# The last two pairs of output blocks move from GpSimd's queue to SP's, as fp32, behind the buffers of earlier transfers

## Chip, cores, metric

One core of one Trainium2 chip. The metric is the device time of one execution in microseconds (us), the median of several runs; lower is better. Every ratio below is the mean time of one kernel's fast runs over that of the other's fast runs of the same rounds, so it is not quite the ratio of the medians that stand beside it.

Three words are used throughout. To *evacuate* a block is to copy a matmul's result out of PSUM, where matmuls leave it, into a buffer in SBUF, from which a transfer can take it. A *closing DRAIN* is an instruction that stands behind an engine's last work in the program; the profile doesn't count it as busy. The *barrier* is the last exchange of semaphores between the engines, which ends only when the last engine has come to it.

## The reference

Attention with a window (plain for four heads, dilated for four) for 8 x 8 x 576 x 64, followed by a soft mixture of experts with 32 slots. Only its last line matters here:

```python
logits = x @ phi                       # x: 4608 x 512, the attention's output
...                                    # slot_out: 32 x 512, from the experts' weights
c = logits - logits.max(1, keepdims=True)
c = np.exp(c)
c /= c.sum(1, keepdims=True) + 1e-09
return (c @ slot_out).astype(np.float32)     # 4608 x 512 fp32, 9.44 MB
```

## The kernel before

All but the end of the kernel is the same before and after. The end multiplies the exponentials `ET` (fp16, 32 slots by 4608 rows) by `so_sb` (the slots' outputs), scales each row by `rrow`, and writes. The 36 blocks of 128 rows go in pairs. Pairs 0 to 7 are written in two halves of 256 columns, because the left half of `so_sb` is ready earlier; pairs 8 to 17 are written whole. Everything is fp16 in SBUF, and GpSimd's transfers cast it to the fp32 of the output.

```python
def combine_full(pair):
    r0 = 256 * pair
    ot = out_pool.tile([128, 2, DMODEL], FP16, name=f"of_{pair}", tag="of", bufs=8)
    for k in range(2):
        blk = 2 * pair + k
        fp = psum_f.tile([128, DMODEL], FP32, name=f"f_{blk}", tag="f")
        nc.tensor.matmul(fp, ET[:, 128 * blk : 128 * blk + 128], so_sb, start=True, stop=True)
        if k == 0:
            nc.scalar.activation(out=ot[:, k, :], in_=fp, func=AF.Copy, scale=rrow[:, blk : blk + 1])
        else:
            nc.vector.tensor_scalar(out=ot[:, k, :], in0=fp, scalar1=rrow[:, blk : blk + 1],
                                    scalar2=None, op0=ALU.mult)
    nc.gpsimd.dma_start(out=out[r0 : r0 + 256, :].rearrange("(k p) n -> p k n", k=2), in_=ot)
...
    # half pairs of the left half, combine(0, pair), stand here (cut)
    for pair in range(NSPLIT // 2, NFIN // 2):            # 8 .. 17
        combine_full(pair)
        if pair >= NFIN // 2 - NSPLIT // 2:               # from 10 on: half pairs 0 .. 7, right half
            combine(1, pair - (NFIN // 2 - NSPLIT // 2))
```

The softmax here doesn't subtract the row's maximum and nothing guards it: scores larger than these inputs give would overflow.

## Time and profile before

| | before |
|---|---|
| time, median of 4 runs | 184.27 us (183.78 to 184.45) |
| span of the profiled execution | 182.06 us |
| output transfers issued by GpSimd (POOL) | 27 |
| last weights used, second copy to `so_sb` | 156.15 us |
| landing of the last output transfer | 178.99 us |
| end of POOL's long closing drain | 181.33 us |

The lines that carry the reading stand in the prediction. Three more fix the two ends of the output stage: the second copy to `so_sb`, after which no input is awaited, and POOL's last two issues. They are from the view of instructions in order of time (start, duration, engine, line, operation, what waited):

```profile
156.15 0.37 ACT L730 CAST so_sb<-so 128x256 f16<-128x256 f32 x1 [0.48 <-PE so L722]
...
171.32 0.72 POOL L802 DMA_DIRECT2D out_dram<-of  x1 [0.62 <-DMA out_dram<-of]
172.03 0.72 POOL L778 DMA_DIRECT2D out_dram<-ot  x1
```

POOL has issued all at 172.75; from there on only transfers run. I use the moment 156.15 as the origin of the end: how early it comes differs from execution to execution, and differences at the end are only comparable when counted from it. Landings are the times at which a transfer's semaphore got its last increment in the trace.

### The profile page before, as it was taken

The numbers are of one execution on the slowest core, as the hardware profiler recorded it, in microseconds if no ns is written. First come the engines' busy times: TensorE is split into PE (matmuls) and PEld (weight loads), VectorE is DVE, ScalarE is ACT, GpSimd is POOL, SyncE is SP. The second block draws the span as 40 slices with busy tenths as digits, with TensorE's granted clock in tenths as the row PEclk, the third lists the DMA queues.
The fourth block names the chain that finished last, engine by engine and source line by source line (L and its number), as shares of the span: only waits on it lengthen the run. The fifth ranks groups of instructions, "written<-read, shape, count | busy, mean of one in ns | idle before, by whom it ended". The sixth has DMA issues, their size and how long they took to land.

```text
span 182.1 us, 5580 instructions
## 1 busy us (share of the span) xinstructions
PE 143.7 (79%) x2464; PEld 85.7 (47%) x2464; DVE 107.5 (59%) x232; ACT 90.4 (50%) x162; POOL 85.2 (47%) x126
## 2 busy tenths in 40 slices
PE   0467977999999999999999999999869848784000
PEld 0234544646646756756756755746353424231000
DVE  4689776675984785885886886526050205697000
ACT  2044354657667566776776776673400205795000
POOL 7954654624534444263351345614412425999700
PEclk9999995699999699999999999999555996999555
DMA  4999999999999999999999999999999999999991
GB/s 61 197 193 208 208 210 213 203 211 217 198 211 216 201 213 217 199 212 214 202 211 214 202 217 213 216 210 214 214 214 213 195 196 183 377 403 409 410 407 32
DMA packets 29527, 40.75 MB, mean 224 GB/s; under 512 B 1856, under 2 KB 19264, under 8 KB 29504
## 3 DMA queue, kind: packets, MB, share of 16 engines
q0 software_dynamic: 29504, 40.41, 117.7%
q8 instruction: 19, 0.31, 0.6%
q14 instruction: 4, 0.03, 0.0%
HBM read 61.93 MB, written 9.44 MB: 392 GB/s over the span
## 4 chain that ended last, share of the span: by engine, by line
DMA 42%; PE 32%; ACT 7%; DVE 6%; POOL 4%; issue 4%; POOLq 1%
DMA w<-in_moe_w_dram 28%; DMA raw<-in_k_dram 10%; ACT p L293 5%; PE lg L408 5%; PE o_p L339 4%; PE sa L282 4%; DMA out_dram<-of 4%; PE sb L271 3%; PE sa L271 3%; DVE qk L245 2%; PE vb L163 2%; PE va L163 2%; PE rd L389 2%; PE u L452 2%; POOL raw L138 1%
## 5 line engine op out<-in xcount | busy, mean ns | idle before, releaser
L293 ACT ACTIVATE p<-sa 128x960 f16<-128x960 f32 (+2 forms) x24 | 21.4, 890 | 31.6 <-PE sb L282 31.1
L339 PEld LDWEIGHTS <-p 128*128 128x128 f16 (+2 forms) x544 | 19.6, 99 | 13.4 <-issue 9.4
L245 DVE STREAM_TRANSPOSE qk<-raw 128x320 uint32<-128x320 uint32 (+1 forms) x32 | 21.5, 677 | 0.3
L293 ACT ACTIVATE p<-sb 128x960 f16<-128x960 f32 (+2 forms) x24 | 21.2, 885 | 0.0
L271 PE MATMUL sa<-masks,ident 128*128 128x480 f16 (+2 forms) x48 | 14.8, 396 | 7.3 <-POOL masks L489 6.2
L236 DVE STREAM_TRANSPOSE qk<-raw 128x576 uint32<-128x576 uint32 x16 | 19.8, 1248 | 0.1
L212 POOL DMA_DIRECT2D w<-in_moe_w_dram x16 | 8.8, 554 | 21.4 <-DMA vs<-in_v_dram 9.9
L408 PE MATMUL lg<-xTd,phi 128*128 128x288 f16 x32 | 18.3, 659 | 0.0
L271 PEld LDWEIGHTS <-ident 128*128 128x128 f16 x96 | 9.3, 108 | 18.3 <-issue 7.2
L282 PEld LDWEIGHTS <-qk 32*128 32x128 f16 x832 | 12.3, 98 | 11.3 <-issue 9.1
L339 PE MATMUL o_p<-v,p 128*128 128x65 f16 (+1 forms) x288 | 16.6, 201 | 1.2 <-ACT v L172 0.7
L282 PE MATMUL sa<-qk 32*128 32x160 f16 (+4 forms) x416 | 16.2, 215 | 0.8 <-DVE qk L236 0.7
L282 PE MATMUL sb<-qk 32*128 32x160 f16 (+4 forms) x416 | 16.3, 215 | 0.0
L361 DVE TENSOR_TENSOR xd<-o_d,rc_d 128x448 f16<-128x448 f32 (+1 forms) x24 | 14.5, 602 | 0.8
L361 DVE TENSOR_TENSOR xp<-o_p,rc_p 128x448 f16<-128x448 f32 (+1 forms) x24 | 14.5, 602 | 0.8
L271 PE MATMUL sb<-masks,ident 128*128 128x480 f16 (+2 forms) x48 | 14.6, 390 | 0.3 <-ACT p L293 0.2
L219 POOL DMA_DIRECT2D w<-in_moe_w_dram x10 | 6.7, 671 | 16.2 <-DMA w<-in_moe_w_dram 9.8
L209 POOL COPY v<-v 32x1024 f16<-32x1024 f16 x8 | 8.3, 1033 | 11.7 <-DVE v L202 9.0
L163 PE MATMUL va<-vs,orders 32*128 32x256 f16 (+1 forms) x96 | 12.1, 289 | 1.0 <-ACT p L293 1.0
L412 ACT ACTIVATE ET<-lg 128x288 f16<-128x288 f32 x16 | 6.6, 410 | 12.5 <-PE lg L408 12.3
L382 ACT COPY xTp<-rp 128x576 f16<-128x576 f16 x16 | 10.4, 650 | 2.2 <-PE rp L377 2.2
L360 DVE RECIPROCAL rc_p<-o_p 128x7 f32<-128x7 f32 (+1 forms) x24 | 4.8, 198 | 10.7 <-PE o_p L339 10.0
(103 smaller groups left out, 277.2 us busy)
## 6 DMA issues: line engine op xcount, KB each, us to landing
w<-in_moe_w_dram POOLq DMA_DIRECT2D x16, 512.0 KB, 16.8
w<-in_moe_w_dram POOLq DMA_DIRECT2D x5, 1024.0 KB, 19.5
out_dram<-of POOLq DMA_DIRECT2D x10, 512.0 KB, 6.2
vs<-in_v_dram POOLq DMA_DIRECT2D x8, 512.0 KB, 16.1
raw<-in_q_dram POOLq DMA_DIRECT2D x7, 576.0 KB, 18.0
raw<-in_k_dram POOLq DMA_DIRECT2D x7, 576.0 KB, 18.5
out_dram<-ot POOLq DMA_DIRECT2D x15, 256.0 KB, 4.9
w<-in_moe_w_dram POOLq DMA_DIRECT2D x8, 256.0 KB, 9.7
```

Source lines behind the costliest of these rows:

```text
L163: nc.tensor.matmul(o.rearrange("p (h d) -> p h d", h=4), l, st[:, 0:4, D * r : D * r + D], start=(r == 0), stop=(r == DIL - 1), skip_group ...
L209: nc.gpsimd.tensor_copy(out=vL[b % NV][0:32, :, :, 0:D], in_=vD[b % NV][96:128, :, :, 0:D])
L212: nc.gpsimd.dma_start(out=w1t[e][:, 2 * i : 2 * i + 2, :].rearrange("p l f -> p (l f)"), in_=moe_w1[e, 256 * i : 256 * i + 256].rearrange( ...
L236: nc.vector.transpose(out=dst, in_=src)
L245: nc.vector.transpose(out=o, in_=i)
L271: nc.tensor.matmul(sps[h // 2][:, h % 2, 0:n], ident, bias[g], start=True, stop=False, skip_group_check=True,)
L282: nc.tensor.matmul(sps[h // 2][:, h % 2, c0 : c0 + w], kt_[32 * h : 32 * h + 32, k0 : k0 + 128, tt], qt_[32 * h : 32 * h + 32, q0 : q0 + w ...
L293: nc.scalar.activation(out=pt, in_=sps[ab][:, :, 0:n], func=AF.Exp, scale=SCALE)
L339: nc.tensor.matmul(o[p0 : p0 + np_, n, :], l, rr, start=(k == 0), stop=(k == len(jobs) - 1), skip_group_check=True,)
L361: nc.vector.tensor_tensor(out=x.rearrange("p t (h d) -> p (t h) d", h=4)[0:nq, u0:u1, :], in0=o[0:nq, 0:n, 0:D], in1=rc[0:nq, 0:n, None].b ...
L382: nc.scalar.copy(out=xTp_t[b][:, c, :], in_=rg)
L408: nc.tensor.matmul(lp, phi4[:, kc].rearrange("p c s -> p (c s)"), rhs, start=(kc == 0), stop=(kc == 3))
```

## The change

The intent: two pairs less for GpSimd's queue, without a cast, and so late that they run behind all of GpSimd's transfers. For that the two last full pairs (16 and 17) share their fp32 buffers with an earlier transfer (pair 15, half pair 5): they can only be evacuated from PSUM when that one has landed. The two last half pairs are moved ahead of them. Fewer buffers for the other tiles make room.

```diff
--- before.py
+++ after.py
@@ -761,7 +761,13 @@
                 stop=True,
                 skip_group_check=True,
             )
-        ot = out_pool.tile([128, 2, NH], FP16, name=f"ot{half}_{pair}", tag=f"ot{half}", bufs=NSPLIT // 2)
+        if (half, pair) == (1, 5):
+            ot = out_pool.tile([128, 2, DMODEL], FP32, name="last1_a", tag="last1")
+            ot = ot[:, 0, 0:NH].bitcast(FP16).rearrange("p (k n) -> p k n", k=2)
+        else:
+            ot = out_pool.tile(
+                [128, 2, NH], FP16, name=f"ot{half}_{pair}", tag=f"ot{half}", bufs=NSPLIT // 2 - half
+            )
         if pair % 2 == 0:
             for k in range(2):
                 blk = 2 * pair + k
@@ -782,7 +788,13 @@
 
     def combine_full(pair):
         r0 = 256 * pair
-        ot = out_pool.tile([128, 2, DMODEL], FP16, name=f"of_{pair}", tag="of", bufs=8)
+        if pair < NFIN // 2 - 3:
+            ot = out_pool.tile([128, 2, DMODEL], FP16, name=f"of_{pair}", tag="of", bufs=6)
+        else:
+            tag = "last1" if pair == NFIN // 2 - 1 else "last0"
+            ot = out_pool.tile([128, 2, DMODEL], FP32, name=f"ol_{pair}", tag=tag)
+            if pair == NFIN // 2 - 3:
+                ot = ot[:, 0, :].bitcast(FP16).rearrange("p (k n) -> p k n", k=2)
         for k in range(2):
             blk = 2 * pair + k
             fp = psum_f.tile([128, DMODEL], FP32, name=f"f_{blk}", tag="f")
@@ -799,7 +811,7 @@
                     scalar2=None,
                     op0=ALU.mult,
                 )
-        nc.gpsimd.dma_start(
+        (nc.gpsimd if pair < NFIN // 2 - 2 else nc.sync).dma_start(
             out=out[r0 : r0 + 256, :].rearrange("(k p) n -> p k n", k=2), in_=ot
         )
 
@@ -813,10 +825,14 @@
             if pair in at:
                 slot_out(1, (HALVED[at[pair]],))
         slot_out(1, HALVED[1:])
-        for pair in range(NSPLIT // 2, NFIN // 2):
+        for pair in range(NSPLIT // 2, NFIN // 2 - 2):
             combine_full(pair)
             if pair >= NFIN // 2 - NSPLIT // 2:
                 combine(1, pair - (NFIN // 2 - NSPLIT // 2))
+        for pair in range(2):
+            combine(1, NSPLIT // 2 - 2 + pair)
+        for pair in range(2):
+            combine_full(NFIN // 2 - 2 + pair)
     psum_f.release()
     psum_so.release()
     out_pool.release()
```

## The prediction

> **What bounds the kernel now.** I read the page first: which engine is full at the end, and what the transfers do there.
>
> ```profile
> POOL 7954654624534444263351345614412425999700
> DMA  4999999999999999999999999999999999999991
> GB/s 61 197 193 208 208 210 213 203 211 217 198 211 216 201 213 217 199 212 214 202 211 214 202 217 213 216 210 214 214 214 213 195 196 183 377 403 409 410 407 32
> ```
>
> A slice is 4.55 us. From slice 35 on the output is written at about 410 GB/s and the transfer engines are full up to slice 39; compute ends before that. Only the end can change: the change touches nothing before the output stage. Next, the end cut into stretches (columns: stretch, its length, busy time of PE, PE loads, DVE, ACT, POOL, clock, DMA share, GB/s):
>
> ```profile
> 172.00:174.00 2.00, 0.00 (x0) 0.00 (x0) 0.00 (x0) 0.00 (x0) 0.75 (x2) 0.50 1.64 407
> 174.00:176.00 2.00, 0.00 (x0) 0.00 (x0) 0.00 (x0) 0.00 (x0) 0.00 (x0) 0.50 1.64 411
> 176.00:178.00 2.00, 0.00 (x0) 0.00 (x0) 0.00 (x0) 0.00 (x0) 0.00 (x0) 0.50 1.48 361
> 178.00:179.00 1.00, 0.00 (x0) 0.00 (x0) 0.00 (x0) 0.00 (x0) 0.00 (x0) 0.50 0.19 38
> 179.00:181.40 2.40, 0.00 (x0) 0.00 (x0) 0.00 (x0) 0.00 (x0) 0.00 (x0) 0.50 0.00 0
> ```
>
> The transfers keep their pace until 177.5 and are over by 179.0, yet the span is 182.1. So some 3 us at the end belong to no transfer and no busy engine. What fills them is in two other views: SP's own waits, and the instructions of the last line of the program (the closing drains and barrier).
>
> ```profile
> SPq L851 <- DMA out_dram<-ot: 178.2, 1, 178.2
> SPq L851 <- PEq L851: 2.6, 2, 2.1
> ...
> L851 POOLq EVENT_SEMAPHORE  x4: 17/17/17, 181.4 to 182.0; - x4
> L851 POOLq DRAIN  x3: 51/86/9513, 171.8 to 181.8; - x3
> ```
>
> SP waits for the last output transfer (the trace's semaphore records put its landing at 178.99), then once more, 2.1 us, in the barrier. The view blames PE, but PE stopped at 166. The engine that comes late to the barrier is POOL: its first closing DRAIN starts at 171.81 and takes 9.513 us, so it ends at 181.33. That is 2.34 us after the last landing. SP was through its own closing waits at 179.38; the barrier then takes 0.73 us (181.33 to 182.06). The tail of 3.07 us after the last landing is therefore 0.39 (SP) + 1.95 (POOL's drain alone) + 0.73 (barrier). This, and not the 410 GB/s, is what the change can shorten.
>
> **What the Trainium skill says.** "DMA: Bandwidth & Descriptors", section "SWDGE vs HWDGE vs iDMA": a DMA that casts must be issued by GpSimd, whose software writes descriptors; DMAs from SP have theirs made by hardware. This agrees with the kernel: all output is fp16 cast to fp32 on POOL, and only fp32 buffers let SP write. Section "Issuing engines are not separate DMA queues": a second issuing engine adds no bandwidth. The trace has one queue alone, so no run yet shows it; I assume it. Section "Latency and other measured facts": first byte after about 0.6 us from SP, 1 us from GpSimd; the trace before has no transfer from SP. "VectorE: DVE Perf Modes", section "The DRAIN you can't avoid", calls the closing drains constant at about 12 ns on all engines. For SP (7 ns) that agrees, for POOL it doesn't: 9513 ns.
>
> **The change part by part.**
>
> *Bytes.* The output in HBM is fp32 both ways; two pairs are 2 x 524,288 B = 1.05 MB, at 409 GB/s 2.56 us. Reading fp32 instead of fp16 from SBUF doubles the read side only. The loads of this kernel, which read fp32 and write fp16, move 214 GB/s written, so 428 GB/s read; the read side has no lower limit than what is needed. I count no gain or loss.
>
> *POOL.* POOL issues 27 output transfers before (2, 15 and 10), 25 after. Each costs it 0.717 us, but its last issue ends at 172.75, six us before its data have landed, so that saving is hidden. What counts is that its last transfer, now the half pair 7, has 1.05 MB less in front of it: it lands at 178.99 - 2.56 = 176.4. If the drain ends 2.34 us after POOL's last landing, it ends at 178.8 instead of 181.33. The drain then lies beside SP's transfers.
>
> *The new wait.* The buffer of pair 16 is that of pair 15, the buffer of pair 17 is that of half pair 5. The trace has pair 15 landing at 174.49 and half pair 5 at 175.18; nothing ahead of them moves (the order of instructions of the changed program has the same sequence on POOL up to there). Evacuations cost as before, from the rows of that tile:
>
> ```profile
> L791 ACT ACTIVATE of<-f,rrow x10: 681/687/695, 157.0 to 165.8; 128x512 f16<-128x512 f32 x10
> L795 DVE TENSOR_SCALAR of<-f,rrow x10: 741/751/751, 157.2 to 165.9; 128x512 f16<-128x512 f32 x10
> ```
>
> Wait 0.04, then ACT 0.69 beside DVE 0.75, then 0.05 to SP: pair 16 is issued at 174.49 + 0.84 = 175.33. The second pair follows: DVE 175.28 to 176.03, issued at about 176.1, while pair 16 is still moving. From issue to first byte I take 0.6 (the skill) to 1.3 us (my doubt): 175.9 to 176.6.
>
> *The hole.* Behind pair 15 POOL's queue still holds three half pairs, 786 KB, 1.92 us. The sixteen transfer engines do not finish together: the increments of one transfer arrive over 0.9 us (175.51 to 176.41 for pair 16 before). The last data packet ends 0.4 us before its landing. So the fast engines run dry at about 175.1, the slowest at 176.0. Against a first byte at 175.9 to 176.6 the slowest engine, which sets the end, loses 0 to 0.6 us; part of the 1.92 us covers the 0.84 of evacuation and the issue.
>
> *The end.* From 176.0 to 176.6, plus 2.56 of data, plus 0.4 receipt: the last landing comes at 179.0 to 179.6, say 179.35; before 178.99. Then SP's closing waits, one more than before, 0.45; then the barrier, 0.73: 180.5. Sum against 182.06: +0.36 for the hole, +0.06 for SP's wait, -1.95 for the drain, so -1.5 us. The executions took 184.23 where the span was 182.1; carried over, 182.7. I add 0.1 for a slower start on SP and say 182.8, which is 0.8% less.
>
> *Smaller parts.* Six buffers instead of eight for full pairs: pair 14 reuses that of pair 8, which lands at 162.3, about when pair 14 is evacuated (162.2); its transfer is issued only at 165.6, so a wait of some tenths is hidden. The SP queue waits, before its first transfer, for all eight semaphores of POOL's transfers; the built program shows counts of 64 to 96 there, where the last outputs bring them to 192 or more, so these are old loads, long landed.
>
> **The rivals.** (1) *The drain doesn't shorten.* It could hold until every transfer of the core has ended, SP's too. Then the end is 179.35 + 2.34 + 0.73 = 182.4, and the time 184.6. For it: only one drain is in the trace, so I can't tell what it waits for. Against: POOL has no part in SP's descriptors. A variant, in which the drain ends a fixed 8.58 us after POOL's last issue, gives 170.7 + 8.6 = 179.3, for POOL's last issue moves forward to about 170.0 (it waits for a transfer that landed at 169.35). SP would still come later; no difference. (2) *A larger hole.* If a transfer from SP takes 2 us from issue to its first byte, the landing comes at 175.33 + 2.0 + 2.56 + 0.4 = 180.3, the end at 181.5 and the time at 183.6. For: the wait, the evacuation and the issue now stand in series where POOL had a backlog. (3) *No hole and better pace.* Transfers without a cast and without software descriptors might run at 428 instead of 409 GB/s, 0.11 us less, and hardware descriptors might level the engines' 0.9 us spread; then the landing is at 178.5 and the time at 182.0. (4) *The output stage is bandwidth bound, so nothing moves.* The page says so at first sight; against it stands the 3 us behind the last byte.
>
> **Range and chances.** Weights: main account about 0.6 (182.2 to 183.3), larger hole 0.2 (183.3 to 184.0), no drain gain 0.12 (184.2 to 184.9), better pace 0.08 (181.7 to 182.2). That gives 182.8 with 182.0 to 184.1. Faster by over 2% means under 180.6: even with the drain wholly hidden and no hole the bound is about 182, so 0.02. Slower by over 2% is over 187.9: 0.01. Within 2%: 0.97.
>
> **What the profile of the changed kernel would show.** Right: POOL's long DRAIN ends near 178.8, before SP is through its waits; ACT and DVE wait for a DMA before each of their last two evacuations; GB/s dips near 175.5 to 176.5; the last landing at 179.0 to 179.6 is of a transfer from SP; the span is near 180.5, with some 1.2 us behind the last landing. Wrong: a DRAIN that ends 2.3 us after SP's landing (rival 1), or a dip of over 1 us in the transfers (rival 2). The whole account fails if the drain's length has to do with neither the landing nor the issue of POOL's last transfer.

## The result

| | before | changed |
|---|---|---|
| median of 4 runs each | 184.27 us | 183.05 us (182.48 to 183.20) |
| ratio, 95% interval | | 0.9932 (0.9904 to 0.9961) |
| span of the profiled execution | 182.06 | 181.38 |
| `so_sb` complete | 156.15 | 156.71 |
| POOL's last landing | 178.99 | 177.11 |
| end of POOL's drain | 181.33 | 179.37 |
| SP's last landing | none | 180.35 |
| `so_sb` to last landing | 22.84 | 23.64 |
| last landing to end | 3.07 | 1.02 |

The changed kernel is 0.7% faster, about 1.25 us (0.0068 of 184.3). Within a margin of 2% that is "the same", but the interval excludes 1. Two further samples on other occasions, in the experiments, gave 0.9896 and 0.9931. The two last rows of the table account for it: +0.80 and -2.05, together -1.25 us.

The page of the changed kernel, the lines that answer to the first ones of the prediction:

```profile
POOL 7954473633633265163371337434401443999600
DMA  4999999999999999999999999999999999999996
GB/s 60 196 196 207 205 212 212 203 211 215 200 213 215 201 212 213 203 212 213 203 211 216 201 215 215 212 212 213 215 213 215 196 196 171 329 386 410 407 319 231
...
q1 hardware_dynamic: 544, 1.05, 1.6%
```

The slices are 4.53 us now. The last slice, nearly empty before (32 GB/s), carries 231 GB/s: the transfers reach closer to the end of the span. The slice ahead of it has fallen from 407 to 319: there is a hole. A second queue has appeared with the 1.05 MB of the two pairs. The hole, cut finer (same columns as in the prediction; the DMA share adds up the packets' times, so it is over 1 where the packets of one transfer engine overlap):

```profile
174.00:175.50 1.50, 0.00 (x0) 0.00 (x0) 0.24 (x1) 0.26 (x1) 0.00 (x0) 0.50 1.93 397
175.50:176.50 1.00, 0.00 (x0) 0.00 (x0) 1.00 (x2) 1.00 (x2) 0.00 (x0) 0.50 0.79 155
176.50:177.00 0.50, 0.00 (x0) 0.00 (x0) 0.17 (x1) 0.08 (x1) 0.00 (x0) 0.50 0.05 8
177.00:178.00 1.00, 0.00 (x0) 0.00 (x0) 0.00 (x0) 0.00 (x0) 0.00 (x0) 0.50 1.00 365
178.00:179.50 1.50, 0.00 (x0) 0.00 (x0) 0.00 (x0) 0.00 (x0) 0.00 (x0) 0.50 1.02 382
```

While ACT and DVE evacuate (175.5 to 176.5, both 1.00 us busy), most transfer engines have run dry, and when SP's transfers come they move 365 to 382 GB/s, not 409. The order of events at the end, from the view in order of time:

```profile
167.98 0.72 POOL L814 DMA_DIRECT2D out_dram<-ol  x1 [0.35 <-issue]
168.69 0.72 POOL L784 DMA_DIRECT2D out_dram<-last_a  x1
169.88 1.43 POOL L784 DMA_DIRECT2D out_dram<-ot  x2 [0.47 <-issue]
175.24 1.34 ACT L803 ACTIVATE ol<-f,rrow 128x512 f32<-128x512 f32 x2 [9.46 <-DMA out_dram<-ol]
175.26 1.41 DVE L807 TENSOR_SCALAR ol<-f,rrow 128x512 f32<-128x512 f32 x2 [9.10 <-DMA out_dram<-ol]
176.09 1.04 SPq L814 DMA_DIRECT2D out_dram<-ol  x2
```

The first line is pair 15, whose landing (175.13) lets ACT and DVE go on after 9.46 and 9.10 us of waiting. SP's two issues follow at 176.09 and 176.75; the first packet starts at 177.01. The closing instructions (count, shortest/median/longest in ns, first and last start):

```profile
L867 SPq EVENT_SEMAPHORE  x8: 17/28/28, 177.2 to 181.3; - x8
...
L867 POOLq DRAIN  x3: 51/91/8817, 170.5 to 181.0; - x3
L867 SPq DRAIN  x3: 7/7/7, 180.4 to 180.7; - x3
```

POOL's long drain starts at 170.55, takes 8.817 us and is over at 179.37, one microsecond before SP's last landing. SP goes through its own closing waits by 180.49 and the barrier follows at once. Before, SP stood 2.1 us in that barrier.

### The profile page after: what moved, and what is told of

It is laid out like the page before. It is cut to its first block, busy times and chain, and to the rows that moved or that the text cites. A ratio compares the mean times of both kernels' runs of the same rounds, so it can differ in the third digit from the quotient of the medians.

```text
span 181.4 us, 5591 instructions
## 1 busy us (share of the span) xinstructions
PE 145.3 (80%) x2464; PEld 86.9 (48%) x2464; DVE 107.3 (59%) x232; ACT 90.6 (50%) x162; POOL 83.7 (46%) x124
## 2 busy tenths in 40 slices
DMA packets 29527, 40.75 MB, mean 225 GB/s; under 512 B 1856, under 2 KB 19264, under 8 KB 29504
## 3 DMA queue, kind: packets, MB, share of 16 engines
q1 hardware_dynamic: 544, 1.05, 1.6%
## 4 chain that ended last, share of the span: by engine, by line
DMA 44%; PE 33%; DVE 6%; ACT 5%; POOL 5%; issue 3%; DVEq 0%; POOLq 0%
DMA w<-in_moe_w_dram 28%; DMA raw<-in_k_dram 10%; PE o_p L339 5%; PE lg L408 5%; PE sa L282 4%; ACT p L293 4%; DMA out_dram<-ol 4%; PE sa L271 4%; PE sb L271 4%; DMA out_dram<-ot 3%; DVE qk L245 2%; PE rd L389 2%; PE vb L163 2%; PE va L163 2%; PE u L452 2%
## 5 line engine op out<-in xcount | busy, mean ns | idle before, releaser
L212 POOL DMA_DIRECT2D w<-in_moe_w_dram x16 | 8.8, 552 | 18.5 <-DMA vs<-in_v_dram 7.4
L271 PE MATMUL sb<-masks,ident 128*128 128x480 f16 (+2 forms) x48 | 15.1, 403 | 0.2 <-ACT p L293 0.2
L219 POOL DMA_DIRECT2D w<-in_moe_w_dram x10 | 6.7, 670 | 15.8 <-DMA w<-in_moe_w_dram 11.3
L227 POOL DMA_DIRECT2D w<-in_moe_w_dram x8 | 6.0, 748 | 11.5 <-DMA w<-in_moe_w_dram 11.5
```

What stands on the lines that cost most here:

```text
L212: nc.gpsimd.dma_start(out=w1t[e][:, 2 * i : 2 * i + 2, :].rearrange("p l f -> p (l f)"), in_=moe_w1[e, 256 * i : 256 * i + 256].rearrange( ...
L271: nc.tensor.matmul(sps[h // 2][:, h % 2, 0:n], ident, bias[g], start=True, stop=False, skip_group_check=True,)
```

## The experiments

The theory: *the gain is POOL's closing drain, which ends some 2.3 us after the landing of POOL's last transfer; the change puts that time beside SP's transfers. The new wait costs, through the hole.* The rivals: the gain comes from SP's queue or the missing cast itself; or from the order of writing; or the drain's length is fixed by POOL's last issue and not by a landing; or the drain waits for all transfers. All outputs were correct. Twelve runs; each ratio is to the kernel before on the same chip. The table at the end of this section gathers them.

### Own buffers: the deferral undone

Against the changed kernel (`w1t` holds weights that are no longer needed):

```diff
-            ot = out_pool.tile([128, 2, DMODEL], FP32, name=f"ol_{pair}", tag=tag)
+            if pair > NFIN // 2 - 3:
+                ot = w1t[pair - (NFIN // 2 - 2)][:, 0:2, :].bitcast(FP32)
+            else:
+                ot = out_pool.tile([128, 2, DMODEL], FP32, name=f"ol_{pair}", tag=tag)
```

> Only the deferral is undone: pairs 16 and 17 get fp32 buffers of their own (in memory of dead weights), so SP can issue them at about 167 instead of 176. Theory (the gain is POOL's closing drain, which ends 2.3 us after POOL's last landing, moved beside SP's transfers): SP's 1.05 MB now travel early, among POOL's, and POOL's last landing moves back to the end of all transfers, about 179.0 to 179.6; the drain ends at about 181.6, the span at 182.0 to 182.6, the time is 184.0 to 184.5, ratio to before 1.00: the gain is lost although the hole of 1.2 us in the transfers is gone. Rival (the gain comes from the hardware queue or the missing cast, the wait only costs): the hole is gone, time about 182, ratio 0.988.

Measured: 184.78 us, ratio 1.0016 (0.9995 to 1.0037). The gain is lost, as the theory said. SP issues at 167.91 and its last transfer lands at 178.33; POOL's last one lands at 180.19. The closing instructions of this run:

```profile
L870 POOLq DRAIN  x3: 51/91/11709, 170.7 to 182.9; - x3
L870 SPq DRAIN  x3: 7/7/7, 180.4 to 182.7; - x3
```

170.74 + 11.71 = 182.45, which is 2.25 us (before rounding) after POOL's last landing, and 10.9 us after its last issue ended (171.60). SP was done at 180.5 and stood in the barrier. So fp32, SP's queue and two POOL issues fewer gain nothing by themselves. What the deferral buys is that POOL is finished first.

### POOL issues the deferred pairs: the queue undone

```diff
-        (nc.gpsimd if pair < NFIN // 2 - 2 else nc.sync).dma_start(
+        nc.gpsimd.dma_start(
```

> Only the queue is undone: the last two pairs stay fp32 and deferred, but POOL issues them. Theory: POOL's last landing is now the last of all, about 180.3; the drain ends 2.3 us later, about 182.6, the span at 183.3, the time about 185.0, ratio 1.004: slower than before by the hole. Variant (the drain ends a fixed 8 us after POOL's last issue, which is at about 177.5 here): drain to 185.6, time about 188. Rival (SP's queue has no part in the gain, the order of writing has): time about 183.1.

Measured: 186.22 us, ratio 1.0100 (1.0071 to 1.0129), slower than expected by 1.2 us. The drain behaves as the theory has it:

```profile
L867 POOLq DRAIN  x3: 51/86/6432, 177.2 to 184.1; - x3
L867 SPq DRAIN  x3: 7/7/7, 181.6 to 183.9; - x3
```

177.18 + 6.43 = 183.61, 2.34 us after the landing at 181.27. POOL's last issue ended at 178.01, 5.6 us before, against 8.6 in the kernel before: a drain fixed by the issue is out. What I had mis-sized is the hole: POOL takes up the issue only at 176.55 (SP at 176.09), its first packet comes 1.30 us after that (SP's 0.92), and between its two landings lie 1.49 us for 512 KB, where a full queue needs 1.28.

### All full pairs by SP

```diff
-        ot = out_pool.tile([128, 2, DMODEL], FP16, name=f"of_{pair}", tag="of", bufs=8)
+        i = pair - NSPLIT // 2
+        ot = w1t[i // 2][:, 2 * (i % 2) : 2 * (i % 2) + 2, :].bitcast(FP32)
...
-        nc.gpsimd.dma_start(
+        nc.sync.dma_start(
```

(against the kernel before)

> All ten full pairs are fp32 in buffers of their own and issued by SP as soon as they are evacuated, without any deferral; the half pairs stay with POOL. Theory: POOL's share ends well before SP's, so its drain is over by the time SP's last transfer lands, and there is no hole: last landing at 179.0 to 179.6, then 0.15 and the barrier 0.85, span 180.0 to 180.6, time 181.7 to 182.3, ratio 0.988. If SP's transfers run at 384 GB/s, as its two did in the changed kernel, against 409 of POOL's, 5.2 MB of them cost up to 0.9 us more: 182.6. Rival (deferral is needed for the gain): 184 or more.

Measured: 185.09 us, ratio 1.0036 (1.0010 to 1.0061). This expectation failed. I had thought that POOL, with the smaller share, would be done well ahead of SP; the trace has POOL's last landing at 180.58 and SP's at 180.45. The two queues ran side by side to the very end, so POOL's drain (end at 182.51) was exposed. Also the pace fell: 390, 387, 375 and 373 GB/s in four slices of the output, against 403 to 410 before. It is the deferral, or whatever else makes POOL finish first, that matters, not how few bytes POOL has.

### The whole output by SP

As above, with the half pairs in fp32 and by SP too (the same edit for the two single blocks of pair 0):

```diff
-        ot = out_pool.tile([128, 2, NH], FP16, name=f"ot{half}_{pair}", ...
+        ot = out_pool.tile([128, 2, NH], FP32, name=f"ot{half}_{pair}", ...
...
-        nc.gpsimd.dma_start(
+        nc.sync.dma_start(
```

> The whole output is fp32 and issued by SP, in the order of the kernel before, without deferral; POOL issues no output at all. Theory: POOL's last landing is then a load, at about 156, its drain is long over, and the end is SP's last landing plus about 1.0 us. If transfers from fp32 by SP keep the 414 GB/s that they showed in the run with earlier buffers (1.05 MB in 2.53 us), the last landing is at about 179.0 to 179.9, the time 182.2, ratio 0.988. If they run at the 383 GB/s of the changed kernel (1.37 us for 512 KB), 9.4 MB take 1.5 us more and the time is 183.7. If the two mixed queues alone made the run with all full pairs on SP slow (373 to 390 GB/s), the first number holds.

Measured: 184.14 us, ratio 0.997 (0.9938 to 1.0002). POOL's last landing is a load at 156.72, and the end comes 1.22 us after SP's last landing at 181.47: no drain in the tail. But that landing comes 24.25 us after `so_sb`, 1.4 us later than in the kernel before, and takes most of the gain back. The second of the three expectations comes nearest (the slow pace, even slower than I took it), and as there is one queue alone, it is not the mixing of two that makes it. The pace in this run, over stretches of 5 us:

```profile
165.00:170.00 5.00, 2.64 (x12) 0.96 (x11) 3.66 (x6) 3.16 (x7) 0.00 (x0) 1.00 1.03 363
170.00:175.00 5.00, 0.00 (x0) 0.00 (x0) 0.00 (x0) 0.00 (x0) 0.00 (x0) 0.53 1.04 370
```

### Earlier buffers

Pair 16 takes the buffer of pair 14, pair 17 that of pair 15; half pair 5 gets an ordinary buffer back.

```diff
-        if (half, pair) == (1, 5):
+        if False:
...
-        if pair < NFIN // 2 - 3:
+        if pair < NFIN // 2 - 4:
             ot = out_pool.tile([128, 2, DMODEL], FP16, name=f"of_{pair}", tag="of", bufs=6)
...
-            tag = "last1" if pair == NFIN // 2 - 1 else "last0"
+            tag = f"last{pair % 2}"
...
-            if pair == NFIN // 2 - 3:
+            if pair < NFIN // 2 - 2:
```

(and `bufs=NSPLIT // 2` for the half pairs)

> Deferral stays, but the buffers come free earlier: pair 16 takes the buffer of pair 14 and pair 17 that of pair 15 (landings at 173.3 and 175.1 instead of 175.1 and 175.8). Theory: the hole closes, SP's last landing comes about 0.9 us earlier, at 179.4; but SP's pair 16 now shares the engines with POOL's last half pairs, whose last landing moves from 177.1 to about 178.0, and its drain ends at about 180.3: span 181.1, time 182.8; so most of the closed hole is given back to the drain. If the drain had no part in it the time would be 182.1.

Measured: 182.18 us, ratio 0.9875 (0.9851 to 0.9898). The hole is closed, and nothing is given back. The stretches that answer to those of the changed kernel:

```profile
175.50:176.50 1.00, 0.00 (x0) 0.00 (x0) 0.72 (x1) 0.64 (x1) 0.00 (x0) 0.50 1.64 404
176.50:177.00 0.50, 0.00 (x0) 0.00 (x0) 0.00 (x0) 0.00 (x0) 0.00 (x0) 0.50 1.08 399
177.00:178.00 1.00, 0.00 (x0) 0.00 (x0) 0.00 (x0) 0.00 (x0) 0.00 (x0) 0.50 1.06 410
...
L867 POOLq DRAIN  x3: 51/91/8864, 170.7 to 180.4; - x3
```

My account of POOL's last landing was wrong: I expected SP's pair 16 to delay it by 0.9 us, to 178.0; it landed at 177.31, 20.35 us after `so_sb`, against 20.40 in the changed kernel. SP issued at 174.48, yet its first packet started at 175.95: it stood behind most of what POOL had already queued, and shared with the rest only up to POOL's last packet at 176.91. So POOL's drain ended at 179.57, still ahead of SP's last landing at 179.84. (In the run with own buffers the same shows more strongly: issued at 167.91, first packet at 171.57.) SP's last landing comes 22.88 us after `so_sb`; before it was 22.84. All of the 3.07 us behind the last landing but 0.88 is gone, and no byte comes later.

### The order alone

The two last half pairs ahead of the two last full pairs, all else as before:

```diff
-        for pair in range(NSPLIT // 2, NFIN // 2):
+        for pair in range(NSPLIT // 2, NFIN // 2 - 2):
             combine_full(pair)
             if pair >= NFIN // 2 - NSPLIT // 2:
                 combine(1, pair - (NFIN // 2 - NSPLIT // 2))
+        for pair in range(2):
+            combine(1, NSPLIT // 2 - 2 + pair)
+        for pair in range(2):
+            combine_full(NFIN // 2 - 2 + pair)
```

> One part of the change alone: the two last half pairs go ahead of the two last full pairs; all stay fp16, issued by POOL, no shared buffers. Every theory in which SP's queue or the drain makes the gain expects the time of before, ratio 1.00 within 0.003; if the order made the gain, 0.993.

Measured: 184.23 us, ratio 0.998 (0.9950 to 1.0009). The interval holds 1 and excludes the 0.993 of the rival. The trace agrees: 22.80 us from `so_sb` to the last landing and 3.07 to the end, as before.

### The changed kernel again

No edit.

> The changed kernel once more, to stand beside the others on the same chip: ratio 0.993.

Measured: 182.84 us, ratio 0.9896 (0.9869 to 0.9923), a little lower than the first 0.9932; the intervals overlap. Its trace repeats the first (23.62 and 1.02 us).

### Three pairs by SP

Pairs 15, 16 and 17 by SP, in buffers of pairs 12, 13 and 14; the half pairs 5, 6 and 7 ahead of them. The core of the edit, against the changed kernel:

```diff
-        if pair < NFIN // 2 - 3:
-            ot = out_pool.tile([128, 2, DMODEL], FP16, name=f"of_{pair}", tag="of", bufs=6)
+        if pair < NFIN // 2 - 6:
+            ot = out_pool.tile([128, 2, DMODEL], FP16, name=f"of_{pair}", tag="of", bufs=4)
...
-            tag = "last1" if pair == NFIN // 2 - 1 else "last0"
+            tag = f"last{pair % 3}"
...
-        (nc.gpsimd if pair < NFIN // 2 - 2 else nc.sync).dma_start(
+        (nc.gpsimd if pair < NFIN // 2 - 3 else nc.sync).dma_start(
```

> Three full pairs go by SP, deferred to the buffers of pairs 12, 13 and 14. Theory: in the run with earlier buffers the drain (end at 179.6) was already hidden behind SP's last landing (179.8), so hiding it deeper gains nothing: the end is set by the bytes of all transfers plus 1.0 us, time 182.2, ratio 0.987 to 0.989, with the drain ending near 178.5. If the drain still cost something there, 181.8 or less.

Measured: 182.86 us, ratio 0.9899 (0.9861 to 0.9936). No better than two pairs with earlier buffers, as the theory has it (the median is 0.6 us above what I wrote, the interval holds my range). One detail was off: the drain ended at 179.53, not near 178.5. SP's first transfer did hold up POOL's last one here: it landed 20.25 us after `so_sb`, hardly sooner than the 20.35 with two pairs on SP, although a whole pair, 1.28 us of data, had left POOL's queue.

### POOL with uncast fp32, and POOL with deferred casts

Two runs to learn whether the slow pace is SP's queue, the missing cast, or the start from idle engines. The first is the run "the whole output by SP" with POOL as the issuer of all output transfers:

```diff
-        nc.sync.dma_start(
+        nc.gpsimd.dma_start(
```

The second is the run "POOL issues the deferred pairs" with those pairs in fp16:

```diff
-            if pair == NFIN // 2 - 3:
-                ot = ot[:, 0, :].bitcast(FP16).rearrange("p (k n) -> p k n", k=2)
+            ot = ot[:, 0, :].bitcast(FP16).rearrange("p (k n) -> p k n", k=2)
```

> The whole output is fp32 in SBUF as in the run with all output on SP, but POOL issues it. It measures the pace of uncast transfers by themselves: 407 to 411 GB/s in the middle of the output if the cast makes no difference and SP's queue was the slow part (367 there); about 367 if reading fp32 from SBUF is the slow part. The drain is exposed as before: time about 184.6 at the first pace (ratio 1.00), about 187 at the second (2.4 us more for 9.4 MB).

Measured: 188.50 us, ratio 1.0217 (1.0191 to 1.0244). Pace:

```profile
165.00:170.00 5.00, 0.99 (x5) 0.29 (x3) 2.10 (x4) 1.47 (x4) 2.82 (x5) 0.86 1.01 338
170.00:175.00 5.00, 0.00 (x0) 0.00 (x0) 0.00 (x0) 0.00 (x0) 3.12 (x6) 0.50 1.01 351
```

Without the cast the transfers are slower, on POOL's queue (338 to 351 GB/s) still more than on SP's (363 to 370). It is the slowest run; whether by over 2% is unclear, as its interval holds 1.02. The cast is not all that differs: without it POOL's queue moved the same bytes in fewer, larger packets. From the pages of the kernel before and of this run (packets, MB, share):

```profile
q0 software_dynamic: 29504, 40.41, 117.7%
q0 software_dynamic: 25152, 40.41, 108.5%
```

And a transfer engine has one packet under way on the mean (DMA share 1.01 here, 1.03 and 1.04 by SP), where with the cast it has 1.64 (the stretches in the prediction). By SP the packets stayed as they were with the cast (29528 in all, 29527 before), so their size is no part of what makes SP slower. On POOL's queue no run separates it from the cast.

> As the run in which POOL issues the two deferred pairs, but these are fp16 and cast, as all others. It separates the two causes of the slow pace after the hole (1.37 us for 512 KB with SP, 1.49 with POOL, against 1.28 in a full queue): 1.28 between the last two landings if the missing cast is slow, 1.4 or more if starting from idle engines is. The time: 0.1 to 0.3 us below that of the fp32 variant (186.2), so about 186.0, ratio 1.009, as the drain is exposed and the hole is there. If the fp32 transfers themselves made the loss of that run, about 184.5.

Measured: 185.94 us, ratio 1.0084 (1.0056 to 1.0111). Between the last two landings, after the hole, lie 1.22 us, where the fp32 variant had 1.49. So on POOL's queue the start from idle engines costs no pace; the missing cast, with the packets that go with it, does. The time is 0.28 us below that of the fp32 variant, as expected, but the two ran on different occasions and their intervals overlap, so this rests on the traces; the rest of the loss is the hole and the exposed drain (2.34 us after the last landing again).

### Earlier buffers against the changed kernel, side by side

No new edit.

> The variant with earlier buffers once more, on one chip with the changed kernel, to settle whether it is the faster of the two. From the traces (last arrival of weights to the end: 23.8 us there, 24.7 us in the changed kernel) it should be 0.9 us faster than the changed kernel: ratio to before about 0.987.

> The changed kernel beside it: ratio to before 0.990 to 0.993, some 0.9 us slower than the variant with earlier buffers.

Measured, on one chip: 182.21 us, ratio 0.9873 (0.9852 to 0.9893) with earlier buffers; 183.14 us, ratio 0.9931 (0.9883 to 0.9980) for the changed kernel. The two intervals touch, but every execution of the first (181.86 to 182.40) is below every one of the second (182.47 to 184.77). The medians differ by 0.93 us, as the traces said. The version with earlier buffers is the fastest.

### All runs, counted from `so_sb`

For one profiled execution of each kernel (the three repeats, left out, agree with these in A + B within 0.14 us): A, from the start of the second copy to `so_sb` to the last landing; B, from there to the end; the difference of A + B to the kernel before (25.91); and the timed difference, ratio minus 1 times 184.6 us. Last column: end of POOL's long drain minus POOL's last landing.

| run | A | B | A+B against before | timed | drain after landing |
|---|---|---|---|---|---|
| before | 22.84 | 3.07 | | | 2.34 |
| changed | 23.64 | 1.02 | -1.25 | -1.26 | 2.26 |
| own buffers | 23.12 | 3.01 | +0.22 | +0.30 | 2.25 |
| POOL issues the deferred, fp32 | 24.56 | 3.23 | +1.88 | +1.85 | 2.34 |
| POOL issues the deferred, cast | 24.30 | 3.23 | +1.62 | +1.55 | 2.34 |
| all full pairs by SP | 24.05 | 2.72 | +0.86 | +0.66 | 1.93 |
| whole output by SP | 24.25 | 1.22 | -0.44 | -0.55 | (1.24, a load) |
| earlier buffers | 22.88 | 0.88 | -2.15 | -2.31 | 2.26 |
| order alone | 22.80 | 3.07 | -0.04 | -0.37 | 2.34 |
| three pairs by SP | 22.97 | 1.02 | -1.92 | -1.86 | 2.22 |
| whole output fp32 by POOL | 27.01 | 3.07 | +4.17 | +4.01 | 2.34 |

Read column B first: it is about 1 us where SP lands last and POOL's drain is hidden, and 2.7 to 3.2 us in every other run. Column A then tells what was paid for it. The two together give the timed difference within 0.35 us in each row.

## Why the prediction was right

The prediction said 182.8 us (range 182.0 to 184.1), 0.8% less; measured were 183.05 us, 0.7% less. The mechanism is the one that it named; the size of the hole is not, and that the number came so near is in part luck, as the sum below shows. Its steps:

- **The tail, not the bandwidth, is what the change can shorten: shown.** The 3.07 us behind the last landing became 1.02. In the run with own buffers, with the same bytes on the same queues, they came back as 3.01.
- **The drain ends 2.34 us after POOL's last landing: shown,** with 1.93 to 2.34 in ten kernels whose POOL transfers land between 177.1 and 183.2. The rival that it depends on the issue falls with the run in which POOL issued last at 178.01 and drained 5.6 us later, and with own buffers, 10.9 us later. The rival that it waits for all transfers falls with the changed kernel itself: the drain ended at 179.37 while SP's landing came at 180.35.
- **POOL's last landing moves forward by 2.56 us: right,** 20.40 us after `so_sb` instead of 22.84, so 2.44.
- **The hole: right in kind, too small in size.** The term was +0.36; A rose by 0.80. Its parts: counted from `so_sb`, SP issues 0.2 us later than I worked out. The first packet started 0.92 us after the issue, in the middle of the 0.6 to 1.3 I allowed. From the first packet to the last landing it took 3.34 us where I had put 2.96 (2.56 of data and 0.4 of receipt). The prediction had 23.20 us from `so_sb` to the last landing (179.35 less 156.15) and its rival 2, the larger hole, 24.15; measured were 23.64, about midway. One of its signs of rival 2, a dip of over 1 us in the transfers, is there too: 155 GB/s from 175.5 to 176.5 and 8 to 177.0. But rival 2's reason, 2 us from SP's issue to its first packet, is not: that was 0.92.
- **"I count no gain or loss" for fp32 against fp16: wrong, and part of the 0.38 us just named.** I argued from the loads, which read fp32 from HBM and not from SBUF, that reading fp32 cannot be the limit. After the same hole, with POOL as issuer, two cast pairs took 3.11 us from the first packet to the last landing (177.61 to 180.72), two fp32 pairs 3.42 (177.85 to 181.27). So a start after the hole takes some 0.15 more than 2.96 even with the cast, and about 0.2 of the 0.38 goes with fp32; this is an estimate, as no run has SP move cast data. The run of the whole output in fp32 moves 363 to 370 GB/s by SP and 338 to 351 by POOL, where cast transfers move 407 to 411 (the stretches of the kernel before in the prediction). Rival 3 of the prediction, a better pace without the cast, has its sign reversed in these runs.
- **The end after the last landing: 1.18 predicted** (0.45 for SP's closing waits, 0.73 for the barrier), **1.02 measured.** Most of SP's closing waits were over before its last landing came: 0.15 us remained, and the barrier took 0.88.
- **The smaller parts: right.** Pair 14's evacuation waited 0.26 us for its buffer, at 163, and its transfer was issued at 166.19 behind POOL's other issues. SP's wait for eight semaphores was long met.

The sum: -1.5 + 0.1 was predicted, -2.05 + 0.80 = -1.25 measured. The hole was 0.44 us larger and the tail shrank 0.16 us more than I had it; these two misses, and the 0.1 put on for SP, partly cancel.

Two things stay open. Why POOL's drain needs about 2.3 us after the landing, no run tells. And uncast transfers are slow in a steady stream, but SP's two fp32 pairs in the run with earlier buffers are not: 1.29 and 1.24 us per 512 KB from landing to landing, and the repeated run had 1.25 between its two. In the changed kernel the same two transfers need 1.35 to 1.37. The runs differ in how far apart the sixteen engines are when the transfers begin (increments of one transfer spread over 0.94 us there, 0.23 here; 0.44 with three pairs, at 1.25 to 1.28 us). The trace of the whole output by SP goes the same way: pairs 8 and 9 land 1.28 us after the transfer ahead of them, with spreads of 0.80 and 0.71, pairs 15, 16 and 17 need 1.40 to 1.44 with 0.33 to 0.44; pair 12, 1.76 with 0.76, falls out of the row. The cast pairs after the hole need only 1.22 at a spread of 0.19, and fp32 by POOL is slow at spreads of 1.1 to 2.3 us too, so the spread alone is not it. Whether it is the cause for SP I did not test.

## What to carry to other kernels

Look at what lies behind the last landing before working on the transfers: here 3 us of a 182 us span, of which 2 were one engine's closing drain and invisible in every busy time. When the last transfer of a kernel is on GpSimd's queue, try to let another queue carry the last stretch of data (two pairs, 2.56 us, did here against a drain that ends 2.3 us after GpSimd's landing), and see that GpSimd's own transfers land first. A transfer that is held back so that it comes last should be released while the other queue still has more than its evacuation and start-up ahead of it (here about 1.9 us, from the landing that releases it to its first packet); otherwise part of the gain goes into a hole.

## What the Trainium skill lacked or had wrong

- "VectorE: DVE Perf Modes", section "The DRAIN you can't avoid", calls the closing drains constant at about 12 ns on all engines. On SP they took 7 ns, but GpSimd's first closing drain took 6.1 to 13.7 us in the kernels in which it issued output. It ends 1.9 to 2.3 us after GpSimd's last transfer has landed (ten kernels), and no page has that time.
- "DMA: Bandwidth & Descriptors", section "Queues, rings and completion order", says that each engine takes turns between the queues it has work for. Once SP's packets come, the trace agrees (own buffers, 172.0 to 173.5: 139 packets of POOL's queue, 144 of SP's). But SP's first packet came 4.11 us (three pairs) and 3.66 us (own buffers) after its issue while POOL's queue was full, 1.47 us with a shorter queue (earlier buffers) and 0.92 us on engines nearly idle (changed kernel). In these runs SP's transfer thus stood behind much of what POOL had already queued, which the page does not lead one to expect; what held it back the traces don't show.
- The same page, section "Latency and other measured facts", gives about 0.6 us to the first byte from SP. From the start of the issuing instruction to the first packet it was 0.92 us on nearly idle engines (changed kernel).
- No page says that a transfer from fp32 in SBUF to fp32 in HBM can be slower than one that casts from fp16: in a long stream 363 to 370 GB/s by SP and 338 to 351 by POOL, against 407 to 411, all counted in bytes written. It need not be: SP's two pairs with earlier buffers moved at 406 to 423 (512 KB in 1.29 and 1.24 us).
